# Attention with a gated MLP on one core: reciprocals spread over the partitions by DMA, and more heads with V stationary

## The chip, the cores and the metric

The kernel runs on one core of a Trainium2 chip. The metric is the device time of one execution in microseconds, the median of three runs. Its engines run side by side, each with its own queue of instructions, and wait for each other by semaphores: TensorE (PE, matmuls), VectorE (DVE), ScalarE (ACT), GpSimd (POOL) and SyncE (SP), which here only issues DMAs. Matmul results land in PSUM; everything else is in SBUF, which has 128 partitions.

## The reference

One row block of attention against a cached K and V, and an MLP that gates it; both read the same layer norm of x. There are 2048 queries, 2048 keys, 32 heads of 128, a model width of 512 and an MLP width of 1792; the types are bf16.

```python
xn = layernorm(x)                                   # [2048, 512]
q  = (xn @ wq)                                      # 32 heads x 128
scores = q @ k_cache.T * 128 ** -0.5                # per head [2048, 2048]
p  = softmax(scores)
o  = p @ v_cache                                    # per head [2048, 128]
s  = concat_heads(o) @ wo                           # [2048, 512]
h  = relu(xn @ w1 + b1) ** 2
g  = silu(h @ w2 + b2)
out = x + s * g
```

## The kernel before

The queries are worked in 4 blocks of 512; block and head together give 128 units, called heads here (g = 0 to 127). A head has 8 steps; each step takes two key tiles of 128. The scores are made transposed (keys on partitions), ScalarE takes the exponential of 128x1024 values into one of 8 buffers of pT, and the sum over keys is left to what follows. No maximum is subtracted. The Python program is a scheduler: it emits each engine's instructions in order, with estimated costs, and puts work without a fixed place (`calm`, `pool_quiet`, `sync_quiet`) where it expects the engine to be free.

```python
# scores of step pi (pi = 8 g + k), then the exponential into pT
for n in range(2):
    tt = 2 * k + n
    t = E(PE, partial(_mm, out=psA[...], lhsT=kT[:, i, tt * P:(tt + 1) * P], rhs=qt_sb[:, g % NQS, :], ...))
t_exp[pi] = E(AC, partial(_act, out=pT[:, pi % NPT, :], in_=psA[...], func=ACT.Exp, scale=SM_SCALE),
              deps=[t, t_PV[pi - NPT] ..., t_part.get(pi - NPT)])
```

P·V is made in one of two ways. In the first ("A", 16 heads before), pT is stationary and V, with a column of ones, moves: 64 matmuls of 129 columns a head. The denominators come out as the 129th column, in the queries' partitions; VectorE copies the result to o_un and takes reciprocals, GpSimd (VectorE for the last three heads) scales it to o_bf, and a transposing DMA makes oT.

In the second ("B", 112 heads before), V is stationary and pT moves: 16 matmuls of 512 columns. The result is already transposed (o_col, copied by ScalarE), but the denominators must be summed over partitions by other engines:

```python
def gen_pv_b(pi):
    ...
    for n in range(2):
        t_PV[pi] = E(PE, partial(_mm, out=bankO(b), lhsT=v_sb[:, i, tt, 0:Dh],
                                 rhs=pT[:, pi % NPT, n * QB:(n + 1) * QB], ...))
    if k == NPR - 1:
        t_free[b] = t_col[m] = E(AC, partial(_act, out=o_col[:, m % NOC, :], in_=bankO(b), func=ACT.Copy), ...)

# a step's sum over keys: either whole on VectorE ...
def den_part(pi):   # d_part 128x32 <- pT 128x1024, TRANSPOSE_TENSOR_REDUCE
# ... or GpSimd adds the two halves first, and VectorE reduces the sum
def part_add(pi):   # GpSimd: h_sum 128x512 <- pT[0:512] + pT[512:1024]
def part_half(pi, x):   # VectorE: d_part 128x16 <- h_sum 128x512

def den_sum(g):     # VectorE: d_sum 128x16 <- d_part
def den_write(g):   # DMA: d_scr (in DRAM) <- d_sum
def den_read(g):    # DMA: d_quad 128x(4x16) <- d_scr: each partition reads its four parts
def den_total(g):   # VectorE: d_rec 128x16 <- d_quad
def den_recip(g):   # VectorE: reciprocal in place
def den_spread(g):  # VectorE: r_all 128x512 <- d_rec, transposed in blocks of 32, each value repeated
    t_spr[m] = E(DV, partial(_transpose32, out=r_all[:], in_=spread),
                 deps=[t_rec[m], t_scale[m - 1] if m else None])
def den_scale(g):   # GpSimd: oT 128x512 <- o_col * r_all
    t_scale[m] = tok_oT[g] = E(GP, partial(_tt, out=oT[:, g % NOT, :], in0=o_col[:, m % NOC, :],
                        in1=r_all[:].rearrange("p b i -> p (b i)"), op=ALU.mult),
            deps=[t_col[m], t_spr[m], ...])
```

Which way a head takes is chosen when its turn comes, by the work that VectorE still owes:

```python
choose(g, FIRST_B <= g < NG - 3 and owed(pi) < OWED and (m < NOC or m - NOC in t_dr))
```

The first three and the last three heads are always of the first way. The products with wo, w1, w2 and wq fill the two psF banks between the steps. At the end the last four row tiles are made; they have two buffers z_t and two buffers out_t, the last tile in three pieces of 256, 128 and 128 columns:

```python
s = jt % 2
t = E(DV, partial(_stt, out=tmp_t[:, s, c0:c1], in0=place, scalar=0.5, in1=g_all[...], ...))      # z_t
t_fin[jt] = t_tmp[s] = E(eng, partial(_tt, out=out_t[:, s, c0:c1], in0=tmp_t[:, s, c0:c1],
                         in1=acc[:, qt, c0:c1], op=ALU.add), deps=[t, t_u[jt], t_outdma[s]])
dma = S.emit_dma(eng, partial(_dma, out=out[...], in_=out_t[:, s, c0:c1]), sl[s], deps=[t_fin[jt]])
```

Of the kernel before, what the change touches and what calls it, by code (L numbers as in the profile page):

```python
# [10 lines left out]
P = 128  # L11
# [73 lines left out]
def _uses_port(name, fn):  # L85
# [3 lines left out]
    if name == "DVE":  # L89
        if f in (_tt, _stt):  # L90
            return _in_sbuf(k["in0"]) and _in_sbuf(k["in1"])
        if f in (_ts, _copy):
# [6 lines left out]
          "d_quad": (1230, 4200)}  # L99
# [201 lines left out]
def bass_recurrent_scan__mha_block_cached__dense_activation_squared_relu__prompt_kernel(  # L301
# [40 lines left out]
    OWED = 9000  # L342
# [16 lines left out]
    NSL, NSW, NQS, NPT, NOT, NOC, NHS = 3, 4, 3, 8, 3 * HC, 3, 3  # L359
# [20 lines left out]
    d_sum = sb("d_sum", [P, 2, NBK], F32)  # L380
    d_quad = sb("d_quad", [P, 2, 4, NBK], F32)
    d_rec = sb("d_rec", [P, 2, NBK], F32)
    r_all = sb("r_all", [P, NBK, 32], F32)
    d_scr = nc.dram_tensor("d_scr", [2, 32, 4 * NBK], F32, kind="Internal").ap()
# [6 lines left out]
    x_ln = sb("x_ln", [P, TPB, D], BF16)  # L391
    xn_t = sb("xn_t", [P, TPB, D], BF16)
    st_t = sb("st_t", [P, TPB, 12], F32)
    mv_t = sb("mv_t", [P, TPB, 2], F32)
    nm_t = sb("nm_t", [P, TPB], F32)
# [3 lines left out]
    warm = sb("warm", [P, P], BF16)  # L399
# [33 lines left out]
    sl_dr = [S.slot(f"dr{i}") for i in range(2)]  # L433

# [22 lines left out]
    t_ones = None  # L457
    for i in range(NSL):
        t_ones = E(GP, partial(_memset, out=v_sb[:, i, :, Dh:Dh + 1], val=1.0))
# [12 lines left out]

    def ln_load(j, i, eng=SP):
        jt = j * TPB + i
        t_xl[jt] = S.emit_dma(
            eng, partial(_dma, out=x_ln[:, i, :], in_=A_x[0, jt * P:(jt + 1) * P, :]), sl_xl[i],
            deps=[t_xn.get(jt - TPB)])
# [3 lines left out]
    def ln_bn(j, i, c0=0, c1=D):  # L481
        jt = j * TPB + i
        k = 6 if c0 else 0
        t_bn[jt] = E(DV, partial(_bn_stats, out=st_t[:, i, k:k + 6], in_=x_ln[:, i, c0:c1]),
                     deps=[t_xl[jt], t_xn.get(jt - TPB), t_xr.get(jt - TPB)])
# [15 lines left out]
    def ln_scale(j, i):  # L501
        jt = j * TPB + i
        t_xn[jt] = E(DV, partial(_ts, out=xn_t[:, i, :], in0=x_ln[:, i, :],
                                 scalar1=mv_t[:, i, 0:1], scalar2=rstd[:, i:i + 1],
                                 op0=ALU.subtract, op1=ALU.mult),
                     deps=[t_xr[jt], t_xnr.get(jt - TPB)])

    def ln_transpose(j, i):
        jt = j * TPB + i
        t_xnr[jt] = tok_xT[j][i] = S.emit_dma(  # L510
            SP, partial(_dmaT, out=xnT[:, :, jt % (2 * TPB) * P:(jt % (2 * TPB) + 1) * P],
                        in_=xn_t[:, i, :]),
            sl_xT[i], deps=[t_xn[jt], t_xuse.get(j - 2)])
        assert j < 2 or n_xuse[j - 2] == NFC + H

    def ln_next(j, i):
        ln_scale(j, i)
        ln_transpose(j, i)

# [38 lines left out]
    def first_transpose(i):  # L558
        for c in range(NDC):
            t_xT[i] = E(PE, partial(_peT, out=bankF(1)[:, 0:256].bitcast(BF16)[:, c * P:(c + 1) * P],  # L560
                                    in_=xn_t[:, i, c * P:(c + 1) * P], ident=ident[:]),
                        deps=[t_xn[i], t_ident, tok_xT[0][i - 1] if i else None],
                        inc=(c == NDC - 1))
        t_xnr[i] = t_xT[i]
# [132 lines left out]
    t_sum = {}  # L697
    t_dw = {}
    t_dr = {}
# [60 lines left out]
    def den_sum(g):  # L760
        m = b_no[g]
        t_sum[m] = E(DV, partial(_reduce, out=d_sum[:, m % 2, :],
                                 in_=d_part[:, m % 2, 0:len(t_parts[g]), :].rearrange(
                                     "p n b -> p b n")),
                     deps=t_parts[g] + [t_dw[m - 2] if m >= 2 else None])

    def den_write(g):
        m = b_no[g]
        dst = bass.AP(tensor=d_scr.tensor, offset=d_scr.offset + m % 2 * P * NBK,
                      ap=[[NBK, 4], [4 * NBK, 32], [1, NBK]])  # L770
        t_dw[m] = S.emit_dma(SP, partial(_dma, out=dst, in_=d_sum[:, m % 2, :]), sl_dw[m % 2],
                             deps=[t_sum[m], t_dr[m - 2] if m >= 2 else None])

    def den_read(g):
        m = b_no[g]
        src = bass.AP(tensor=d_scr.tensor, offset=d_scr.offset + m % 2 * P * NBK,
                      ap=[[0, 4], [4 * NBK, 32], [1, 4 * NBK]])
        t_dr[m] = S.emit_dma(SP, partial(_dma, out=d_quad[:, m % 2].rearrange("p a b -> p (a b)"),
                                         in_=src), sl_dr[m % 2],
                             deps=[t_dw[m], t_tot[m - 2] if m >= 2 else None])  # L780

    def den_total(g):
        m = b_no[g]
        t_tot[m] = E(DV, partial(_reduce, out=d_rec[:, m % 2, :],
                                 in_=d_quad[:, m % 2].rearrange("p a b -> p b a")),
                     deps=[t_dr[m], t_spr.get(m - 2)])

    def den_recip(g):
        m = b_no[g]
        t_rec[m] = E(DV, partial(_recip, out=d_rec[:, m % 2, :], in_=d_rec[:, m % 2, :]),  # L790
                     deps=[t_tot[m]])

    def den_spread(g):
        m = b_no[g]
        base = d_rec[:, m % 2, :]
        spread = bass.AP(tensor=base.tensor, offset=base.offset,
                         ap=[list(base.ap[0]), [1, NBK], [0, 32]])
        t_spr[m] = E(DV, partial(_transpose32, out=r_all[:], in_=spread),
                     deps=[t_rec[m], t_scale[m - 1] if m else None])

    def den_scale(g):
        m = b_no[g]
        t_scale[m] = tok_oT[g] = E(
            GP, partial(_tt, out=oT[:, g % NOT, :], in0=o_col[:, m % NOC, :],
                        in1=r_all[:].rearrange("p b i -> p (b i)"), op=ALU.mult),
            deps=[t_col[m], t_spr[m], t_wodone[g - NOT] if g >= NOT else None])
# [5 lines left out]
    tiles = {}  # L812
    WEIGHT = {den_part: 1130, part_half: 610, den_sum: 350, den_total: 170, den_recip: 130,
              den_spread: 600}
# [4 lines left out]
    def plan_b(g):  # L819
        tiles[g] = 0  # L820
        first = NPR * g
        for k in range(NPR):
            calm(first + k + NPT - 2, partial(den_part, NPR * g + k))
        calm(first + NPR + 6, partial(den_sum, g))
        sync_quiet.append(partial(den_write, g))
        sync_quiet.append(partial(den_read, g))
        calm(first + NPR + 12, partial(den_total, g))
        calm(first + NPR + 12, partial(den_recip, g))
        calm(first + NPR + 13, partial(den_spread, g))
        pool_quiet.append(partial(den_scale, g))  # L830

    def needs(fn):
# [6 lines left out]
        if f in (den_sum, den_total, den_recip, den_spread, den_scale, den_write, den_read):  # L839
            g = a[0]  # L840
            m = b_no[g]
            if f is den_sum:
                if tiles[g] < NPR:
                    return None
                return t_parts[g] + [t_dw.get(m - 2) if m >= 2 else t_parts[g][0]]
            if f is den_write:
                return [t_sum.get(m), t_dr.get(m - 2) if m >= 2 else t_sum.get(m)]
            if f is den_read:
                return [t_dw.get(m), t_tot.get(m - 2) if m >= 2 else t_dw.get(m)]
            if f is den_total:  # L850
                return [t_dr.get(m), t_spr.get(m - 2) if m >= 2 else t_dr.get(m)]
            if f is den_recip:
                return [t_tot.get(m)]
            if f is den_spread:
                return [t_rec.get(m), t_scale.get(m - 1) if m else t_rec.get(m)]
            return [t_col.get(m), t_spr.get(m)]
# [17 lines left out]
    def ready_at(fn):  # L874
        toks = needs(fn)
        if toks is None or any(t is None for t in toks):
            return None
        slack = SLACK if fn.func in (den_total, den_read) else 0
        return S.ready(toks) + slack
# [25 lines left out]
    def fill_pool(until):  # L905
        while GP.t < until:
# [6 lines left out]
            if x < NHS or t_half[x - NHS] is not None:  # L913
# [125 lines left out]
    def at(step, fn):  # L1039
        events.setdefault(step, []).append(fn)  # L1040
# [86 lines left out]
    def job_wo(j, m, qt, c0=0, c1=D):  # L1127
# [16 lines left out]
        def evac(bank, step):  # L1144
# [14 lines left out]
            if last:  # L1159
# [5 lines left out]
                      deps=[box[0], t_g[jt], t_tmp[s], t_zrd[s]])  # L1165
                eng = GP if j == NQB - 1 and qt in (0, 2) else DV
                t_fin[jt] = t_tmp[s] = E(
                    eng, partial(_tt, out=out_t[:, s, c0:c1], in0=tmp_t[:, s, c0:c1],
                                 in1=acc[:, qt, c0:c1], op=ALU.add),
                    deps=[t, t_u[jt], t_outdma[s]])  # L1170
# [3 lines left out]
                                 in_=out_t[:, s, c0:c1]), sl[s], deps=[t_fin[jt]])  # L1174
# [5 lines left out]
    def load_xt(jt):  # L1180
        if jt < NQB * TPB:
            tok_xt[jt] = S.emit_dma(
                GP, partial(_dma, out=x_t[:, jt % 2, :], in_=A_x[0, jt * P:(jt + 1) * P, :]),
                sl_xt[jt % 2], deps=[t_u[jt - 2] if jt >= 2 else None])
# [141 lines left out]
    for j in range(NQB):  # L1326
        if j + 1 < NQB:
            for i in range(TPB):
                at(j * SPB + 3 * NPR, partial(ln_load, j + 1, i))
# [59 lines left out]
    t_bankF[:] = [t_q0[3], tok_xT[0][3]]  # L1389
    gen_pv(3)  # L1390
# [9 lines left out]
    for pi in range(NPAIR):  # L1400
        g, k = divmod(pi, NPR)
        if k == 0 and g > 0:
# [81 lines left out]
```

## Time and profile before

| | |
|---|---|
| median of 3 runs | 1221.58 us (1221.49 to 1221.91) |
| span of the profiled execution | 1219.6 us |
| TensorE busy | 1212.7 us |
| ScalarE, VectorE, GpSimd busy | 1088.4, 1076.8, 1067.4 us |
| moved by DMA | 174.83 MB, DMA engines busy about 0.7 of the span |

A line of the groups names the source line (often a helper's), the engine, the operation, what is written and read, the count, the busy time in us and the mean in ns of one; behind the second bar stands the idle time of the engine just before these instructions, and what ended it. The chain of waits follows the last instruction of the execution back to what released it, step by step; a piece of it is given as start, duration, engine and tile. Ends of matmuls are modelled, so a full TensorE is judged by the starts of its matmuls.

### The profile page before, as it was taken

Reading aid. Unit: us, or ns where it says so; the run is one execution under the profiler, and the core shown is the slowest. Engines: PE = TensorE matmul, PEld = TensorE weight load, DVE = VectorE, ACT = ScalarE, POOL = GpSimd, SP = SyncE. Lnnn points to the kernel's source line nnn. Section 1 sums busy time; section 2 is a strip of 40 time slices with the busy share of each in tenths; the row PEclk is TensorE's granted clock in tenths of the full one; section 3 lists DMA queues with packets and bytes.
Section 4 is the critical chain, followed back from the end, with each engine's and each line's share of the span. In section 5 each row is a group of like instructions: output and inputs, shape, how many; then the busy total and the mean of one; then the engine's idle time right before and its main releaser. Section 6 shows DMA issues by size and latency. Waiting matters only on the chain.

```text
span 1219.6 us, 19351 instructions
## 1 busy us (share of the span) xinstructions
PE 1212.7 (99%) x6509; PEld 588.5 (48%) x6509; DVE 1076.8 (88%) x1820; ACT 1088.4 (89%) x1156; POOL 1067.4 (88%) x978
## 2 busy tenths in 40 slices
PE   9999999999999999999999999999999999999998
PEld 7544444445454454444554444444454544444455
DVE  4798999898989888999999989898999899889983
ACT  7898999998988989999898999998989999989994
POOL 1789999998978989999888899999989789899971
PEclk9999999999999999999999999999999999999999
DMA  9998876667777666776687686766666686677651
GB/s 223 186 245 174 178 172 125 131 136 145 132 155 149 137 133 130 142 137 123 139 148 165 130 139 144 137 129 130 145 137 133 133 160 126 133 135 145 122 119 31
DMA packets 655492, 174.83 MB, mean 143 GB/s; under 512 B 642176, under 2 KB 654208, under 8 KB 655392
## 3 DMA queue, kind: packets, MB, share of 16 engines
q1 hardware_dynamic: 653296, 169.52, 70.4%
q0 software_dynamic: 1424, 3.81, 1.1%
q8 instruction: 52, 0.85, 0.3%
q14 instruction: 48, 0.39, 0.1%
q10 hardware_dynamic: 672, 0.26, 0.1%
HBM read 100.27 MB, written 3.01 MB: 85 GB/s over the span
## 4 chain that ended last, share of the span: by engine, by line
PE 96%; DVE 2%; POOL 1%; issue 0%; DMA 0%; ACT 0%; ACTq 0%; POOLq 0%; DVEq 0%
PE psA L226 35%; PE psO L226 31%; PE psF L226 25%; PE psO L231 4%; POOL h_sum L239 1%; DVE d_part L286 1%; DVE acc L249 0%; PE psA L231 0%; DMA out_dram<-out_t 0%; ACT pT L235 0%; DVE out_t L239 0%; POOL oT L239 0%; DVE z_t L249 0%; DVE acc L239 0%; PE psF L270 0%
## 5 line engine op out<-in xcount | busy, mean ns | idle before, releaser
L235 ACT ACTIVATE pT<-psA 128x1024 bf16<-128x1024 f32 x1024 | 1036.6, 1025 | 110.5 <-PE psA L226 71.8
L239 POOL TENSOR_TENSOR h_sum<-pT 128x512 f32<-128x512 bf16 x764 | 867.1, 1164 | 35.8 <-ACT pT L235 15.0
L226 PE MATMUL psA<-qt_sb,kT 128*128 128x512 bf16 x2032 | 604.5, 379 | 1.0 <-ACT pT L235 1.0
L286 DVE TRANSPOSE_TENSOR_REDUCE d_part<-h_sum 128x16 f32<-128x512 f32 x764 | 506.1, 685 | 31.8 <-POOL h_sum L239 29.3
L226 PE MATMUL psO<-pT,v_sb 128*128 128x512 bf16 x1792 | 533.0, 379 | 0.0
L226 PEld LDWEIGHTS psA<-qt_sb,kT 128*128 128x128 bf16 x2032 | 193.5, 98 | 213.1 <-ACT pT L235 4.3
L226 PEld LDWEIGHTS psO<-pT,v_sb 128*128 128x128 bf16 x1792 | 175.3, 98 | 211.4 <-issue 1.2
L239 POOL TENSOR_TENSOR oT<-o_col,r_all 128x512 bf16<-128x512 f32 x112 | 144.7, 1292 | 30.8 <-DVE r_all L290 30.4
L226 PE MATMUL psF<-xnT,wq_sb 128*128 128x512 bf16 (+1 forms) x520 | 168.9, 374 | 0.2 <-DVE xnT L253 0.2
L226 PE MATMUL psF<-wo_all,oT 128*128 128x512 bf16 x480 | 163.7, 379 | 0.0
L286 DVE TRANSPOSE_TENSOR_REDUCE d_part<-pT 128x32 f32<-128x1024 bf16 x132 | 159.1, 1212 | 4.5 <-ACT pT L235 4.1
L253 DVE CAST qt_sb<-psF 128x512 bf16<-128x512 f32 (+1 forms) x130 | 87.0, 669 | 23.4 <-PE psF L226 21.1
L231 PEld LDWEIGHTS psO<-v_sb,pT 128*128 128x128 bf16 x1024 | 68.1, 98 | 28.9 <-ACT pT L235 0.6
L226 PEld LDWEIGHTS psF<-xnT,wq_sb 128*128 128x128 bf16 x520 | 50.3, 98 | 60.0 <-issue 0.3
L231 PE MATMUL psO<-v_sb,pT 128*128 128x129 bf16 x1024 | 78.6, 220 | 0.3 <-ACT pT L235 0.3
L290 DVE STREAM_TRANSPOSE r_all<-d_rec 128x512 f32<-128x512 f32 x112 | 76.8, 686 | 0.5
L226 PE MATMUL psF<-xnT,w_sb 128*128 128x512 bf16 x224 | 77.1, 379 | 0.0
L226 PEld LDWEIGHTS psF<-wo_all,oT 128*128 128x128 bf16 x480 | 46.9, 98 | 56.4
L226 PE MATMUL psF<-w_sb,h2T 128*128 128x512 bf16 x224 | 73.6, 379 | 0.0
L235 ACT ACTIVATE o_col<-psO 128x512 f32<-128x512 f32 x112 | 66.3, 592 | 0.0
L245 DVE TENSOR_SCALAR r_t<-psF,b1f 128x512 bf16<-128x512 f32 x56 | 41.2, 735 | 15.6 <-PE psF L226 14.3
L282 DVE TENSOR_REDUCE d_sum<-d_part 128x16 f32<-128x144 f32 (+3 forms) x112 | 43.1, 385 | 1.1
(59 smaller groups left out, 404.5 us busy)
## 6 DMA issues: line engine op xcount, KB each, us to landing
v_sb<-in_A_v_cache_dram SPq DMA_DIRECT2D x127, 512.0 KB, 4.5
wq_sb<-in_A_wq_dram SPq DMA_DIRECT2D x127, 128.0 KB, 2.5
wo_all<-in_A_wo_dram SPq DMA_DIRECT2D x4, 1024.0 KB, 6.1
w_sb<-in_B_w_dram SPq DMA_DIRECT2D x14, 256.0 KB, 4.4
d_quad<-d_scr SPq DMA_DIRECT2D x112, 32.0 KB
x_t<-in_A_x_dram POOLq DMA_DIRECT2D x16, 128.0 KB, 3.5
kT<-in_A_k_cache_dram SPq DMA_TRANSPOSE x127, 4.7
x_ln<-in_A_x_dram SPq DMA_DIRECT2D x15, 128.0 KB, 3.0
```

What stands on the lines that cost most here:

```text
L226: return e.matmul(out, lhsT, rhs, start=start, stop=stop)
L231: return e.matmul(out, lhsT, rhs, start=start, stop=stop, skip_group_check=True)
L235: return e.activation(out, in_, func, bias=bias, scale=scale)
L239: return e.tensor_tensor(out, in0, in1, op)
L245: return e.tensor_scalar(out, in0, scalar1=scalar1, scalar2=scalar2, op0=op0, op1=op1)
L253: return e.tensor_copy(out, in_)
L282: return e.tensor_reduce(out, in_, axis=AX.X, op=ALU.add)
L286: return e.tensor_reduce(out, in_, axis=AX.X, op=ALU.add, apply_transpose=True)
L290: return e.transpose(out, in_)
```

## The change

In the way with V stationary the reciprocals no longer go to all partitions by a transpose on VectorE. The totals are made in 32 partitions only, one row per 16 queries; the reciprocals are written to a small array in DRAM (r_scr, one value per query) and read back by a second DMA that gives all 128 partitions the same 512 values. Before that, a small transpose on VectorE (128x32) makes d_sum's rows contiguous for its write. r_all gets two buffers, o_col four.

The constants of the scheduler are changed too: OWED from 9000 to 8000, GpSimd takes a step's sum only if VectorE owes more than 3500, and the estimates wait longer for the new reads. With them it chooses the second way for 118 heads in place of 112. To find room, the layer norm has two buffers in place of four (the first block's third and fourth tile borrow x_t and out_t), and the warm-up matmuls read o_bf. The last row tile's result goes to x_t, not to out_t, so that it has its own buffer.

```diff
-    NSL, NSW, NQS, NPT, NOT, NOC, NHS = 3, 4, 3, 8, 3 * HC, 3, 3
+    NSL, NSW, NQS, NPT, NOT, NOC, NHS = 3, 4, 3, 8, 3 * HC, 4, 3
-    OWED = 9000
+    OWED = 8000
+    POOL_OWED = 3500
+    HALF_SLACK = 600
...
+    def den_turn(g):
+        t_row[m] = E(DV, partial(_transpose32, out=d_row[:, m % 2, :], in_=d_sum[:, m % 2, :]),
+                     deps=[t_sum[m], t_dw.get(m - 2)])
...
     def den_read(g):
-        src = bass.AP(..., ap=[[0, 4], [4 * NBK, 32], [1, 4 * NBK]])
+        src = bass.AP(..., ap=[[NBK, 32], [32 * 32, 4], [1, NBK]])     # into 32 partitions
...
-    def den_spread(g):
-        t_spr[m] = E(DV, partial(_transpose32, out=r_all[:], in_=spread),
-                     deps=[t_rec[m], t_scale[m - 1] if m else None])
+    def rec_write(g):
+        t_rw[m] = S.emit_dma(SP, partial(_dma, out=r_scr[m % 2]..., in_=d_rec[0:32, m % 2, :]),
+            sl_rw[m % 2], deps=[t_rec[m], t_spr.get(m - 2)])
+    def rec_read(g):
+        src = bass.AP(tensor=r_scr.tensor, ..., ap=[[0, P], [1, QB]])
+        t_spr[m] = S.emit_dma(SP, partial(_dma, out=r_all[:, m % 2, :], in_=src), sl_rr[m % 2],
+                              deps=[t_rw[m], t_scale.get(m - 2)])
...
-            if x < NHS or t_half[x - NHS] is not None:
+            if (x < NHS or t_half[x - NHS] is not None) and owed(now[0]) > POOL_OWED:
...
+                end = jt == NQB * TPB - 1
+                row = (x_t if end else out_t)[:, s, c0:c1]
-                    eng, partial(_tt, out=out_t[:, s, c0:c1], in0=tmp_t[:, s, c0:c1],
+                    eng, partial(_tt, out=row, in0=tmp_t[:, s, c0:c1],
                                  in1=acc[:, qt, c0:c1], op=ALU.add),
-                    deps=[t, t_u[jt], t_outdma[s]])
+                    deps=[t, t_u[jt], None if end else t_outdma[s]])
```

## The prediction

> **What bounds the kernel now.** I read the page first: busy time and the slices, then the chain of work that ended last.
>
> ```profile
> PE 1212.7 (99%) x6509; PEld 588.5 (48%) x6509; DVE 1076.8 (88%) x1820; ACT 1088.4 (89%) x1156; POOL 1067.4 (88%) x978
> ...
> PEclk9999999999999999999999999999999999999999
> ...
> PE 96%; DVE 2%; POOL 1%; issue 0%; DMA 0%; ACT 0%; ACTq 0%; POOLq 0%; DVEq 0%
> PE psA L226 35%; PE psO L226 31%; PE psF L226 25%; PE psO L231 4%; POOL h_sum L239 1%; DVE d_part L286 1%; DVE acc L249 0%; PE psA L231 0%; DMA out_dram<-out_t 0%; ACT pT L235 0%; DVE out_t L239 0%; POOL oT L239 0%; DVE z_t L249 0%; DVE acc L239 0%; PE psF L270 0%
> ```
>
> TensorE is busy 99% of the span at the full clock and is 96% of the chain. A busy TensorE need not stream without gaps, so I took the starts of its matmul records in the trace. Start to start, a matmul with 512 columns takes 215.8 ns and one with 129 columns 56.7 ns. From 17 us on, only four gaps exceed the usual distance by over 30 ns: 0.10 us at 356, 1.20 us at 904.6, 0.05 us at 1182, 0.44 us at 1202.9. The stream of matmuls is the time; the rest is about 11 us of start and end. The other three engines, at 88 to 89%, count only where they make TensorE wait.
>
> Next the groups by line and shape, for the prices of what comes and goes (mean ns after the comma):
>
> ```profile
> L239 POOL TENSOR_TENSOR h_sum<-pT 128x512 f32<-128x512 bf16 x764 | 867.1, 1164 | 35.8 <-ACT pT L235 15.0 <-DVE d_part L286 13.9 <-DVE d_rec L257 2.7
> ...
> L286 DVE TRANSPOSE_TENSOR_REDUCE d_part<-pT 128x32 f32<-128x1024 bf16 x132 | 159.1, 1212 | 4.5 <-ACT pT L235 4.1
> L239 POOL TENSOR_TENSOR oT<-o_col,r_all 128x512 bf16<-128x512 f32 x112 | 144.7, 1292 | 30.8 <-DVE r_all L290 30.4
> ...
> L290 DVE STREAM_TRANSPOSE r_all<-d_rec 128x512 f32<-128x512 f32 x112 | 76.8, 686 | 0.5
> ...
> L235 ACT ACTIVATE o_col<-psO 128x512 f32<-128x512 f32 x112 | 66.3, 592 | 0.0
> ```
>
> The removed transpose costs VectorE 76.8 us in all, and GpSimd waits 30.4 us for it. Does TensorE ever wait for those? The chain in order of time, around its one long gap (start, us, what):
>
> ```profile
> 901.55 0.63 DVE r_all L290
> ...
> 902.26 1.15 POOL oT L239
> ...
> 903.49 1.16 POOL h_sum L239
> ...
> 904.73 1.03 ACT pT L235
> ...
> 905.81 0.60 PE psA L226 x2
> ```
>
> Once. VectorE was late with the spread of the reciprocals, GpSimd scaled late, hence added late, the exponential waited to overwrite that tile of pT, and the scores waited for the exponential: 1.2 us. Last, the end of the same chain:
>
> ```profile
> 1210.80 1.27 DVE out_t L239
> ...
> 1212.09 3.21 DMA out_dram<-out_t
> ...
> 1215.39 0.44 DVE out_t L239
> ...
> 1216.96 0.29 DVE out_t L239
> ```
>
> The last row tile has the buffer of the tile two before it, and its first piece waits until that tile's output DMA has landed (1215.30). TensorE's last matmul starts at 1215.12; the last VectorE result is there at 1217.25, its DMA is issued at 1217.28.
>
> **What the Trainium skill says.** (1) "TensorE: Matmul & The Clock Gate", section "Wait — 56ns, not 53.3ns?": warm matmuls follow each other at N ÷ 2.4 GHz plus about 2.5 ns. That makes 215.8 ns for 512 columns and 56.3 for 129; the trace has 215.8 and 56.7. It agrees. (2) "SBUF — State Buffer", section "Terms": VectorE and GpSimd take one port pair as an exclusive lock for a whole instruction, and the loser blocks. The trace agrees: GpSimd's out_t ran 1210.24 to 1211.51, and VectorE's out_t, begun at 1210.80, took 1262 ns in place of about 690. (3) "DMA: Bandwidth & Descriptors", section "Anatomy of one DMA — SWDGE (gpsimd) path": about 2 us per DMA are fixed, mostly the receipt of the write. The trace has something near on another queue: a read of d_scr that waits for its write is issued at the earliest 1.94 us after it.
>
> **The change part by part.**
>
> Six heads more with V stationary: 118 instead of 112. With pT stationary a head's P·V is 64 matmuls × 56.66 ns = 3.626 us; with V stationary 16 × 215.84 ns = 3.454 us. The difference is 0.173 us, and × 6 it is 1.04 us. It lies on TensorE, so it counts whole. Order and number of the other matmuls only move.
>
> VectorE: minus 112 transposes, 76.8 us. Minus 12 evictions o_un at 418 ns and 6 reciprocals at 163 ns, 6.0 us. Plus 118 transposes of 128x32 (den_turn); the nearest small VectorE rows, 230 and 234 ns for totals and reciprocals, make 0.17 us an estimate, 20 us. Plus 6 each of d_sum, total and reciprocal, 385 + 230 + 234 ns, 5 us. The built program has 764 half-tile sums (h_sum) as before, and 180 whole-tile sums on VectorE instead of 132: 48 × 1212 ns = 58.2 us. Total 1076.8 − 82.8 + 83.2 = about 1077 us. So all VectorE time won is spent on the six heads' denominators, and none of it shows as time.
>
> GpSimd: 6 × 1292 ns more for oT, 6 × 1040 ns less for o_bf: plus 1.5 us. ScalarE: 6 × 592 ns for o_col: plus 3.6 us. Neither becomes the bound; at 1092 and 1069 us they stay 120 us below TensorE.
>
> DMA: 118 reads of r_all, 128 rows of 2 KB = 256 KB each, 31 MB more on 175 MB; and 118 tiny writes of r_scr. The head's chain becomes write, read, total, reciprocal, write, read, scale. The added pair costs an estimated 5 to 6 us: 2 us for the write as for d_scr, 3 to 4 for the read, between the 3.0 us of the 128 KB x_ln and the 4.5 us of the 512 KB v_sb. A fourth o_col buffer covers that: a head lasts about 9.4 us, so one buffer more is worth more than the added latency. In SyncE's in-order queue the issues grow from 635 us (554 ns for a small one) by about 140 us. K is issued at the median 17 us, at the least 7.6 us, before its first use and lands in 4.7, so delays of 2 to 3 us stay hidden.
>
> The tail: the last tile's pieces write x_t, so the wait until 1215.30 is gone. Now the pieces follow TensorE, but the port lock stands in the way. GpSimd's sum for tile 14 runs 1213.55 to 1214.81. The first piece's z_t ends at 1214.01; its sum then blocks to 1214.81 and needs 0.28 us more (424 ns less the start-up that is hidden, as 547 of 690 ns remained in the earlier case): 1215.09. Then z_t, sum, z_t, sum at 0.33 us each: 1216.41. Against 1217.25 that is 0.84 us won. If VectorE is not blocked, the last piece follows the last matmul (1215.34 at the end) by 0.66 us, and 1.2 us are won.
>
> In sum: 1.04 + 0.84 = 1.9 us. 1221.6 − 1.9 = 1219.7. The gap of 1.2 us at 904 came through r_all on VectorE; I give it 6 in 10 to vanish (−0.7), and put +0.3 for new short gaps, since VectorE is as full as before. That is 1219.3 us.
>
> **The rivals.** (a) The freed 77 us shorten the kernel: then 1150 to 1200. The 99% of TensorE and four gaps of together 1.8 us speak against it; there is nothing to win beyond them. (b) The DMA takes the place of the transpose as a wait: GpSimd now waits for r_all to land, and as it runs in order, each late landing can repeat the gap of 904. SyncE already waited 115.6 us for d_scr to land. For it speaks the longer chain; against it, that the order puts the scale behind other sums (6 to 8 h_sum between two scales at the end), and that d_quad's landing cost VectorE only 0.6 us once. Ten such gaps would make 1231. (c) The tail gains nothing, because tile 14's output, in the old slot of tile 12, ends last: its DMA is issued at 1214.84 and lands about 2 us later, at 1216.8, before the last piece's, which would be issued at 1216.4. Then 0.84 us would shrink, not vanish: 1220. (d) The six heads fill VectorE so that evictions of psF and psO come late: a few gaps of 0.5 to 1 us, 1221 to 1224.
>
> **Range and chances.** The first two terms are sure to about 0.4 us, which makes 1219.3 to 1220.1 with the gap and 1218.1 to 1218.9 without it. Some new gaps stretch it upward. I take 1218.0 to 1221.3. Two per cent are 24 us; the floor of TensorE forbids it downward, and upward it takes twenty gaps like the one of 904. Hence 0.01 faster, 0.98 same, 0.01 slower.
>
> **What would show it.** TensorE at 99% and about 1 us less busy; 1888 matmuls psO with 512 columns and 640 with 129. VectorE near 1077 us, its STREAM_TRANSPOSE at about 0.17 us ×118, and 180 sums from pT. GpSimd's waits for r_all from VectorE gone, some for the DMA in their place. About 205 MB moved, a DMA share near 80%. At the end, the first piece of x_t stretched to about 1 us beside GpSimd's out_t. The prediction is wrong if waits of TensorE for ScalarE add up to over 2 us, or if GpSimd waits for r_all for tens of us and h_sum follows late.

## The result, and the profile after

The changed kernel takes 1225.01 us (median of 6 runs, 1223.39 to 1226.02) against 1221.53 us before (6 runs, 1221.28 to 1222.15). The ratio is 1.0026, with a 95% interval of 1.0013 to 1.0038: 3.5 us slower, where the prediction had 2.2 us faster. The spread is wider too: 2.6 us from the fastest to the slowest run of the changed kernel, 0.9 us before.

The page of the changed kernel, its busy times and the chain of work that ended last:

```profile
PE 1206.5 (99%) x6103; PEld 574.9 (47%) x6221; DVE 1083.0 (89%) x1874; ACT 1090.7 (89%) x1162; POOL 1066.4 (87%) x979
...
DMA packets 679300, 203.53 MB, mean 166 GB/s; under 512 B 650881, under 2 KB 662913, under 8 KB 679201
...
PE 79%; DVE 14%; POOL 3%; DMA 2%; issue 1%; ACT 1%; ACTq 0%; SPq 0%; POOLq 0%; DVEq 0%
PE psA L226 29%; PE psO L226 27%; PE psF L226 20%; DVE d_part L286 8%; POOL h_sum L239 3%; PE psO L231 2%; DVE acc L249 2%; DMA d_quad<-d_scr 1%; DVE qt_sb L253 1%; DVE d_sum L282 1%; ACT pT L235 0%; DVE acc L239 0%; DVE g_all L249 0%; DMA r_scr<-d_rec 0%; POOL oT L239 0%
```

TensorE is still busy 99%, but its share of the chain fell from 96% to 79%; VectorE rose from 2% to 14%. A busy share does not show this, the chain does. (Of 6221 matmuls 6103 have a record; each has its weight load, so the starts can still be read and the missing ones allowed for.) After the first 17 us TensorE's gaps, that is start-to-start distances less N/2.4 + 2.5 ns, add up to 7.7 us; before the change they were 2.3 us. The seven longest of over 0.45 us lie at 134 (0.47 us), 313 (2.12), 328 (0.56), 922 (0.59), 962 (1.00), 1163 (0.77) and 1183 (0.56).

Groups of the changed kernel, those that came or moved:

```profile
L239 POOL TENSOR_TENSOR oT<-o_col,r_all 128x512 bf16<-128x512 f32 x118 | 151.3, 1283 | 33.5 <-DMA r_all<-r_scr 32.0 <-DVE d_part L286 1.3
...
L249 DVE SCALAR_TENSOR_TENSOR acc<-acc,g_all 128x512 f32<-128x512 f32 x16 | 34.2, 2137 | 0.0
...
L282 DVE TENSOR_REDUCE d_rec<-d_quad 32x16 f32<-32x64 f32 x118 | 26.1, 221 | 12.4 <-DMA d_quad<-d_scr 12.3
L290 DVE STREAM_TRANSPOSE d_row<-d_sum 128x32 f32<-128x32 f32 x118 | 23.2, 197 | 2.4
```

The big transpose is gone and a 197 ns one has come. But VectorE now stands idle 12.3 us before the totals, waiting for d_quad to land, that is for its bytes to be there after the DMA was issued (0.6 us, once, before). And the 16 gate products acc = 0.5·acc·g_all, which the diff doesn't touch, cost 34.2 us instead of 26.0.

The chain of the changed kernel around the gap at 962 (start, us, what):

```profile
954.94 5.19 DMA d_quad<-d_scr
...
960.15 0.25 DVE d_rec L282
...
961.15 1.16 DVE d_part L286 x2
962.31 0.59 DVE z_t L249
...
962.95 0.39 PE psF L226
```

d_quad took 5.19 us to land. VectorE runs in order and waited; behind the wait stood the eviction of a psF bank (z_t), and TensorE waited for that bank. The gap at 134 has the same form, with a landing of 4.54 us at 117 and VectorE behind from then on.

The other kind, at 313: VectorE's and then GpSimd's timeline of the changed kernel (start, us, engine, instruction):

```profile
309.42 4.44 DVE L249 SCALAR_TENSOR_TENSOR acc<-acc,g_all 128x512 f32<-128x512 f32 x1
313.78 0.74 DVE L245 TENSOR_SCALAR r_t<-psF,b1f 128x512 bf16<-128x512 f32 x1
```

```profile
307.60 4.48 POOL L239 TENSOR_TENSOR h_sum<-pT 128x512 f32<-128x512 bf16 x4
312.05 1.26 POOL L239 TENSOR_TENSOR oT<-o_col,r_all 128x512 bf16<-128x512 f32 x1
313.94 1.15 POOL L239 TENSOR_TENSOR acc<-acc,x_t 128x512 f32<-128x512 f32 x1 [0.63 <-DVE acc L249]
```

A gate product that took 0.64 us at best took 4.44 us here: it ended 0.55 us after GpSimd's adds and the scale behind them had run through. Both have two operands in SBUF, and I read this as the fight for the shared port pair that the prediction describes. The eviction r_t behind it came late, and TensorE waited 2.1 us.

And the end, where the change did what it was meant to do (chain):

```profile
1214.22 3.92 PE psA L226 x26
...
1218.16 0.44 DVE z_t L249
...
1218.62 0.93 DVE x_t L239
...
1220.69 0.29 DVE x_t L239
```

The wait for the earlier tile's output is gone. The first piece stretched to 0.92 us beside GpSimd's out_t, as foreseen. From the start of TensorE's last matmul (1219.69) to the last VectorE result it is 1.29 us, against 2.13 us before.

### The profile page after: what moved, and what is told of

The parts are those of the page before. It is cut to its first block, busy times and chain, and to the rows that moved or that the text cites. A ratio compares the mean times of both kernels' runs of the same rounds, so it can differ in the third digit from the quotient of the medians.

```text
span 1222.9 us, 19101 instructions
## 1 busy us (share of the span) xinstructions
PE 1206.5 (99%) x6103; PEld 574.9 (47%) x6221; DVE 1083.0 (89%) x1874; ACT 1090.7 (89%) x1162; POOL 1066.4 (87%) x979
## 4 chain that ended last, share of the span: by engine, by line
PE 79%; DVE 14%; POOL 3%; DMA 2%; issue 1%; ACT 1%; ACTq 0%; SPq 0%; POOLq 0%; DVEq 0%
PE psA L226 29%; PE psO L226 27%; PE psF L226 20%; DVE d_part L286 8%; POOL h_sum L239 3%; PE psO L231 2%; DVE acc L249 2%; DMA d_quad<-d_scr 1%; DVE qt_sb L253 1%; DVE d_sum L282 1%; ACT pT L235 0%; DVE acc L239 0%; DVE g_all L249 0%; DMA r_scr<-d_rec 0%; POOL oT L239 0%
## 5 line engine op out<-in xcount | busy, mean ns | idle before, releaser
L226 PE MATMUL psA<-qt_sb,kT 128*128 128x512 bf16 x1980 | 593.3, 379 | 4.3 <-ACT pT L235 1.2
L226 PE MATMUL psO<-pT,v_sb 128*128 128x512 bf16 x1851 | 553.5, 379 | 1.9
L226 PEld LDWEIGHTS psO<-pT,v_sb 128*128 128x128 bf16 x1888 | 184.7, 98 | 222.2 <-issue 0.7
L286 DVE TRANSPOSE_TENSOR_REDUCE d_part<-pT 128x32 f32<-128x1024 bf16 x180 | 217.0, 1209 | 5.7 <-ACT pT L235 5.2
L239 POOL TENSOR_TENSOR oT<-o_col,r_all 128x512 bf16<-128x512 f32 x118 | 151.3, 1283 | 33.5 <-DMA r_all<-r_scr 32.0
L253 DVE CAST qt_sb<-psF 128x512 bf16<-128x512 f32 (+1 forms) x130 | 85.6, 659 | 21.9 <-PE psF L226 19.9
L231 PEld LDWEIGHTS psO<-v_sb,pT 128*128 128x128 bf16 x640 | 42.4, 98 | 17.6 <-ACT pT L235 0.6
L231 PE MATMUL psO<-v_sb,pT 128*128 128x129 bf16 x640 | 49.0, 220 | 0.3 <-ACT pT L235 0.3
L282 DVE TENSOR_REDUCE d_sum<-d_part 128x16 f32<-128x160 f32 (+3 forms) x118 | 46.6, 395 | 1.5
L249 DVE SCALAR_TENSOR_TENSOR h2T<-psF,b1f,r_t 128x512 bf16<-128x512 f32 x56 | 41.8, 747 | 1.7
```

The lines of the kernel that those rows point to most:

```text
L226: return e.matmul(out, lhsT, rhs, start=start, stop=stop)
L231: return e.matmul(out, lhsT, rhs, start=start, stop=stop, skip_group_check=True)
L239: return e.tensor_tensor(out, in0, in1, op)
L249: return e.scalar_tensor_tensor(out=out, in0=in0, scalar=scalar, in1=in1, op0=op0, op1=op1)
L253: return e.tensor_copy(out, in_)
L282: return e.tensor_reduce(out, in_, axis=AX.X, op=ALU.add)
```

## The experiments

Two theories stood first. L: landings are late, VectorE waits for d_quad in order and is then late with PSUM. F: the six more heads fill VectorE again, and that alone makes it late. The table has all runs; "waits" are those of VectorE for d_quad, "gate" is the time of the 16 gate products on VectorE, "gaps" are TensorE's after 17 us. These three are read in the profiled execution, which in e3, e5, e9 and e11 took 0.9 to 2.5 us more than the median. In all sessions the kernel before had medians of 1221.5 to 1221.8 us.

| run | heads with V stationary | us | ratio to before (95%) | waits us (times) | gate us | gaps us |
|---|---|---|---|---|---|---|
| before | 112 | 1221.53 | | 0.6 (1) | 26.0 | 2.3 |
| changed | 118 | 1225.01 | 1.0013 to 1.0038 | 12.3 (13) | 34.2 | 7.7 |
| e1_tail | 112 | 1220.40 | 0.9981 to 0.9997 | 0.2 (1) | 26.0 | 2.3 |
| e2_heads112 | 112 | 1227.05 | 1.0031 to 1.0055 | 21.6 (20) | 22.6 | 8.3 |
| e3_landing | 119 | 1231.46 | 1.0058 to 1.0089 | 4.0 (3) | 32.0 | 16.0 |
| e4_thin | 118 | 1220.36 | 0.9982 to 0.9994 | none | 30.4 | 3.2 |
| e5_gate | 118 | 1218.73 | 0.9964 to 0.9982 | 10.6 (10) | on GpSimd | 2.7 |
| e6_tail_gate | 112 | 1218.92 | 0.9968 to 0.9985 | none | on GpSimd | 1.0 |
| e7_half | 118 | 1219.51 | 0.9976 to 0.9990 | 5.8 (6) | 27.4 | 2.6 |
| e8_half_gate | 118 | 1217.99 | 0.9958 to 0.9981 | none | on GpSimd | 0.8 |
| e9_half_gate_112 | 112 | 1219.02 | 0.9971 to 0.9987 | 8.0 (9) | on GpSimd | 1.7 |
| e10_landing_gate | 119 | 1220.87 | 0.9984 to 1.0000 | 6.4 (7) | on GpSimd | 3.2 |
| e11_nogate | 118 | 1218.41 | 0.9971 to 0.9985 | 7.4 (9) | 19.1 | 3.8 |
| e12_thin112 | 112 | 1219.33 | 0.9977 to 0.9990 | 2.0 (5) | 19.9 | 1.0 |

**e1: the tail alone**, put into the kernel before.

```diff
+                end = jt == NQB * TPB - 1
+                row = (x_t if end else out_t)[:, s, c0:c1]
-                    deps=[t, t_u[jt], t_outdma[s]])
+                    deps=[t, t_u[jt], None if end else t_outdma[s]])
```

> The kernel before with one part of the change alone: the last row tile in its own buffer. Every theory: the wait for the landing of an earlier tile's output goes, 112 heads and four gaps of TensorE stay. From the last matmul's start to the end 3.2 us in place of 4.45 us; 1220.3 us in all (1219.9 to 1220.8).

1220.40 us, 1.36 us less than the kernel before beside it (1221.76). The gaps are those of before, even that at 904. So this part is a gain, and the loss comes from the rest.

**e2: 112 heads, everything else as changed.**

```diff
-            choose(g, FIRST_B <= g < NG - 3 and owed(pi) < OWED and ...)
+            choose(g, g not in [0, 1, 2, 8, 30, 36, 45, 62, 66, 73, 95, 102, 109, 125, 126, 127])
```

> The changed kernel with the same 112 heads as before with V stationary, all else as changed. Theory L (late landings: VectorE, in order, waits for d_quad, is then late with its PSUM evictions, and TensorE waits for the bank): the two more DMAs are still there, so waits for d_quad of about 12 us in all, gaps of TensorE of about 7 us, 1224 to 1226 us. Theory F (the six more heads fill VectorE again, and landings have little to do with it): gaps as before, about 2.3 us, and with the tail's gain 1220.0 to 1221.2 us.

1227.05 us: slower still, and above the range of L too. F falls in its simple form, as VectorE is less full here (busy 1036.6 us against 1083.0) and the kernel slower. The waits for d_quad went up to 21.6 us. Where VectorE has less queued work, the total comes up sooner after its read and more often finds it not landed: the median from landing to the total is 1.2 us here, 1.6 us in the changed kernel. The gate products took only 22.6 us here, less than before the change, so slower gate products didn't make these gaps. Not all come from d_quad: ahead of the one at 365 (1.06 us) GpSimd stood 6.4 us waiting for r_all.

**e4: the same order of instructions with little traffic.**

```diff
-                      ap=[[0, P], [1, QB]])
-        t_spr[m] = S.emit_dma(SP, partial(_dma, out=r_all[:, m % 2, :], in_=src), ...)
+                      ap=[[0, 8], [1, QB]])
+        t_spr[m] = S.emit_dma(SP, partial(_dma, out=r_all[0:8, m % 2, :], in_=src), ...)
```

> The changed kernel with every instruction of TensorE, VectorE and ScalarE in the same order, but r_all's read brings 8 of the 128 partitions only (16 KB in place of 256 KB; the others keep ones, so this leaves the scaling out there): 29 MB less on the DMA engines. L by traffic: d_quad lands as before the change (median 2.6 us in place of 3.25), VectorE's waits for it under 4 us, 1220 to 1222 us. L by SyncE's in-order queue (d_quad is issued late because SyncE stands waiting for r_scr): landings a little shorter, but the waits stay over 8 us and the time at 1223 to 1225 us. F: unchanged, 1224 to 1226 us.

1220.36 us, in the range of L by traffic. TensorE, VectorE and ScalarE have the very same sequence. From the view of the tile d_quad, first of the changed kernel, then of e4:

```profile
its engine sat idle before it (us, times) until:
  DMA d_quad<-d_scr: 12.3, 13
...
DMA to landing us min/median/max: 1.5/3.3/6.9
```

```profile
DMA to landing us min/median/max: 1.5/2.7/5.4
```

With 29 MB less on the DMA engines d_quad's landing falls from 3.3 to 2.7 us in the median (2.6 us before the change, where it was a read of 32 KB instead of 8), VectorE never waits for it, and of the seven long gaps five are gone. d_scr's landing falls too, from 2.9 to 1.9 us. SyncE's order is the same here, and the median from d_scr's landing to d_quad's issue is even longer (2.6 us against 1.3 us), so the gain did not come there. A part of the delay the queue has all the same: ahead of the changed kernel's gap at 1163, d_quad could be issued only when r_scr had landed (chain of the changed kernel):

```profile
1151.38 4.08 DMA r_scr<-d_rec
...
1155.85 3.27 DMA d_quad<-d_scr
...
1159.14 0.26 DVE d_rec L282
```

No run changed SyncE's order alone. The thin read also cut GpSimd's wait for r_all, from 32.0 to 9.5 us, so this run doesn't tell the two waits apart. What stays in e4 are the gap at 313, 1.8 us, with its gate product of 4.45 us, and the one behind it at 328, 0.57 us.

**e12: the thin read with e2's 112 heads**, both edits together; as in e4, the scaling of the other 120 partitions is left out.

> e2 (112 heads, changed chain, 1227 us) with the thin read of e4 and the same order of VectorE. If the bytes of r_all made e2 slow too: waits for d_quad fall from 21.6 us to under 8 us, TensorE's gaps from 8.3 to under 4 us, 1220.5 to 1222.5 us. If the order of 112 heads itself is bad: over 1224 us.

1219.33 us against e2's 1227.05: the traffic made e2 slow as well, and even more so. Waits 2.0 us, gaps 1.0 us. It came out below the range given.

**e7: half the bytes, the same rows.**

```diff
-    r_all = sb("r_all", [P, 2, QB], F32)
+    r_all = sb("r_all", [P, 2, QB], BF16)
-r_scr = nc.dram_tensor("r_scr", [2, QB], F32, kind="Internal").ap()
+r_scr = nc.dram_tensor("r_scr", [2, QB], BF16, kind="Internal").ap()
-        t_rec[m] = E(DV, partial(_recip, out=d_rec[0:32, m % 2, :], in_=d_rec[0:32, m % 2, :]),
+        t_rec[m] = E(DV, partial(_recip, out=d_inv[0:32, m % 2, :], in_=d_rec[0:32, m % 2, :]),
```

> The changed kernel with the same order of instructions, but reciprocals in bf16 from the reciprocal on: r_all's read is 128 KB in place of 256 KB, rows of 1 KB. If landings follow the bytes, this lies between the changed kernel and the thin read: d_quad's median 2.9 to 3.1 us, VectorE's waits for it 5 to 9 us, 1222 to 1223.5 us. If the count of rows matters and not the bytes (128 rows as before, the thin read had 8): as the changed kernel, 1224 to 1226 us.

d_quad's median of 3.0 us and VectorE's waits of 5.8 us lie in the ranges given, so the landings follow the bytes and not the count of rows. The time, 1219.51 us, is 2.5 us below the range, and below e4, which has no waits at all: time does not go with the sum of the waits. One thing more changed here: with r_all in bf16 GpSimd's scale takes 1167 ns in place of 1283, 13.8 us less in all, and the gate products 27.4 us in place of 34.2. How much of the gain is due to that isn't shown; the same holds for e8 and e9.

**e3: estimates of landings raised in the scheduler.**

```diff
-"d_scr": (530, 2200), "d_quad": (530, 4200), "r_scr": (530, 2200), "r_all": (1230, 4400)
+"d_scr": (430, 3000), "d_quad": (430, 5400), "r_scr": (580, 3300), "r_all": (350, 4400)
-    OWED = 8000
+    OWED = 9000
```

> The changed kernel with the scheduler's estimates of landings set near what its trace shows (d_scr 3.0, d_quad 5.4, r_scr 3.3 us; OWED back to 9000), 119 heads with V stationary: VectorE is fuller still, but its work that needs a landing stands later in its order. L: waits of VectorE for d_quad under 3 us in all, TensorE's gaps under 4 us, 1219.0 to 1221.5 us. F: gaps as in the changed kernel or longer, 1224 us or more.

Half a miss for L. The waits fell to 4.0 us (under 3 was expected), yet the time rose to 1231.46 us, with gaps of 16.0 us, of which some 3 us are half clock. Two gaps of 2.8 and 2.5 us stand behind gate products (2.2 us at 312, 2.4 us at 613) and late sums, and each was followed by 3.4 us at half clock (last section). So late landings are not the only cause, and a second theory came up: the fight for the port pair, in a VectorE that has no time left to catch up.

**e5 and e6: the gate products on GpSimd**, in the changed kernel and, with the tail, in the kernel before. The factor 0.5 moves into the evictions of acc. The heads with V stationary are fixed to those of the kernel that each starts from.

```diff
-                t_acc[qt] = t = E(DV, partial(_copy, out=acc[:, qt, :], in_=place),
+                t_acc[qt] = t = E(DV, partial(_ts, out=acc[:, qt, :], in0=place, scalar1=0.5, ...op0=ALU.mult),
-                t_acc[qt] = t = E(DV, partial(_tt, ... in1=acc[:, qt, :], op=ALU.add),
+                t_acc[qt] = t = E(DV, partial(_stt, ... scalar=0.5, in1=acc[:, qt, :], op0=ALU.mult, op1=ALU.add),
-        t_ug[jt] = E(DV, partial(_stt, out=acc[:, qt, :], in0=acc[:, qt, :], scalar=0.5, in1=g_all[...], ...),
+        t_ug[jt] = E(GP, partial(_tt, out=acc[:, qt, :], in0=acc[:, qt, :], in1=g_all[...], op=ALU.mult),
```

> The changed kernel, 118 heads, with the 16 gate products acc times g_all moved from VectorE to GpSimd (the factor 0.5 goes into the evictions of acc before them), so that they can't fight GpSimd for the port pair. The late landings stay. If the lock of 4.4 us at 309 made the 2.1 us gap there: that gap goes, the waits for d_quad stay near 12 us, TensorE's gaps fall from 7.7 to 5 to 6 us, 1222 to 1224 us. If the gap there was made by the landings too: it stays, 1224.5 to 1226 us.

> The kernel before (112 heads, reciprocals spread by VectorE) with the last tile's own buffer and the gate products on GpSimd. The gap of 1.2 us at 904 followed a gate product of 2.3 us; if the lock made it, it goes: TensorE's gaps 1.0 to 1.3 us in all, 1218.8 to 1219.6 us, faster than either kernel. If a full VectorE made it, it only moves: 1220 to 1221 us.

e5 comes to 1218.73 us, 6.3 us under the changed kernel and far below the range. The waits for landings are still there (waits of e5: who for whom, us, times, longest):

```profile
POOL oT L239 <- DMA r_all<-r_scr: 33.0, 14, 6.7
...
DVE d_rec L282 <- DMA d_quad<-d_scr: 10.6, 10, 2.2
```

10.6 us of waits on VectorE and 33.0 us on GpSimd cost little once the gate products are off VectorE: gaps 2.7 us. Most of what is left, 1.2 us at 250 to 258, stands behind another product of two SBUF operands on VectorE, g_all from th_t and z_t, that was not moved: one took 5.01 us, where the quickest took 0.62. e6 shows the same on the kernel before: the gap at 904 is gone, 1218.92 us as expected. In the chain of the kernel before, two gate products stood ahead of that gap:

```profile
891.78 2.98 DVE acc L249
...
897.52 2.22 DVE acc L249
```

**e11: the gate products cut to 8 of 512 columns, order unchanged.** e5 had changed VectorE's order as well (191 whole sums in place of 180); this run does not.

```diff
+    if out.tensor.name == "acc":
+        out, in0, in1 = out[:, 0:8], in0[:, 0:8], in1[:, 0:8]
```

> The changed kernel, every engine's instructions in the same order, full 256 KB reads, but each of the 16 gate products works on 8 of its 512 columns (this leaves the gate out of the other columns), so that it holds VectorE and the port pair for about 0.1 us. If the lock is the second cause beside the landings: waits for d_quad stay at 8 to 14 us, the gap of 2.1 us at 313 goes, 1219.5 to 1222 us. If the landings alone do it: the gap at 313 may go, but gaps at 134, 962 and 1163 stay and the time is 1222.5 us or more.

1218.41 us and waits of 7.4 us, both below the ranges: cutting the gate gives more than taking away the traffic (1220.36 in e4). But the products still took 19.1 us in all, in place of 34.2. At 0.15 and 0.64 us when free, that is an estimated 8 us less work and only 7 us less waiting, 17 us in place of 24, so this run doesn't tell how much of the gain is the lock. The gap at 313 halved (1.05 us) but stayed, and VectorE's and GpSimd's timelines of this run say why (this kernel's lines stand two lower):

```profile
309.53 3.91 DVE L251 SCALAR_TENSOR_TENSOR acc<-acc,g_all 128x8 f32<-128x8 f32 x1
```

```profile
307.72 4.47 POOL L239 TENSOR_TENSOR h_sum<-pT 128x512 f32<-128x512 bf16 x4
312.16 1.26 POOL L239 TENSOR_TENSOR oT<-o_col,r_all 128x512 bf16<-128x512 f32 x1
```

Eight columns, 146 ns when free, took 3.91 us. At this gap the wait costs, not the product. The runs of this kernel fall into two heaps, 13 of 21 from 1217.6 to 1218.8 us and 8 from 1220.3 to 1221.8; the profiled execution is of the upper one (1220.91 us). That one landing more or less decides a gap fits this, but isn't shown.

**e8, e9: both cures, with 118 and with 112 heads.** **e10: e3 with the gate on GpSimd.**

> Both in the changed kernel, 118 heads: bf16 reciprocals and the gate products on GpSimd. If the two causes add, TensorE's gaps come to 2 to 4 us and the time to 1219.5 to 1221.5 us. If VectorE is too full for 118 heads whatever is taken away (F), it stays over 1223 us.

> e8 (bf16 reciprocals, gate products on GpSimd) with the 112 heads of before in place of 118. With landings and lock out of the way, the six heads should be worth what their matmuls say, 6 x 0.173 = 1.04 us: TensorE's gaps under 1.5 us, 1218.7 to 1219.5 us. If 112 heads need other waits than 118 (as e2 was slower than the changed kernel), gaps of 3 us or more, over 1220.5 us.

> e3 (landing estimates near the trace, 119 heads, full 256 KB reads) with the gate products on GpSimd. In e3 the waits for d_quad were short (4.0 us) and the time was 1231 us all the same. If the lock of the gate products made its gaps: they fall from 16 us to under 3 us, 1217.5 to 1219.5 us. If 119 heads with the longer chain are too much for VectorE whatever the lock does: over 1222 us.

e8 is the fastest of all, 1217.99 us, below the range given, a ratio of 0.9969 to before. The page of e8, busy times and chain:

```profile
PE 1211.0 (100%) x6221; PEld 575.5 (47%) x6221; DVE 1058.0 (87%) x1858; ACT 1091.5 (90%) x1162; POOL 1058.2 (87%) x984
...
PE 99%; DMA 0%; DVE 0%; ACT 0%; ACTq 0%; SPq 0%; issue 0%; DVEq 0%
```

TensorE is 99% of the chain again, and the gaps are down to 0.8 us. The cures do not add (5.5 and 6.3 us alone, 7.0 us together): each removes nearly the same gaps. e9 is 1.03 us slower than e8, as six heads should cost. Against e6, which has the tail and the gate moved but the old transpose and 112 heads, the rest of the change is worth 0.9 us in e8 and 0.2 us in e5. e10 brings e3's gaps from 16.0 to 3.2 us, so most of them came with the gate on VectorE. Its 1220.87 us are above the range; with 119 heads and full reads some gaps stay.

## Why the prediction was wrong, point by point

- **Six heads more, 1.04 us on TensorE:** right in the size. e8 against e9 gives 1.03 us. That it is so close is partly luck: e9 still has 8.0 us of waits, and its profiled execution 0.9 us more gaps than e8's. The start of TensorE's last matmul less the gaps, 1212.3 us in e8 and 1213.1 in e9, gives 0.9.
- **The tail, 0.84 us:** right in its mechanism, with the stretched first piece (0.92 us), and to the last VectorE result exactly 0.84 us. The span's end gained 0.4 us more, as the span ended 1.9 us after that result instead of 2.3; e1 has 1.36 us in all.
- **VectorE stays full, at 1077 us:** 1083 us. The terms were right (d_part from pT 217 us; d_row 197 ns against an estimated 170). What was missing are 8 us more of gate products, by waiting and not by work.
- **DMA:** 203.5 MB and a share near 81%, as said; r_all lands in 3.8 us, as estimated. The write of r_scr was put too low: 3.2 us in the median, not 2, so the added pair takes about 7 us, not 5 to 6. SyncE's issues grew from 635 to 862 us, not by about 140. "Delays of 2 to 3 us stay hidden" was argued for K alone, and wasn't carried over to the small reads that share the DMA engines. There it fails. Before, nine tenths of the totals began 1.07 us or more after d_quad had landed; after the change that figure is 0.02 us, and in e4 1.16 us.
- **"+0.3 for new short gaps, since VectorE is as full as before":** this is the step that failed. The gaps went from 2.3 to 7.7 us, +5.4, where the prediction had −0.4 with its share for 904; without 904 the new gaps come to over 6 us. As full as before did not mean as much in time: d_quad came later, and the gate products lost more to GpSimd. Rival (b), the DMA as a wait in place of the transpose, was named, but put aside in part because "d_quad's landing cost VectorE only 0.6 us once", a figure of the old traffic. Its sign came true, 32.0 us of GpSimd's waits for r_all, but that wait is not what stood ahead of the long gaps in the changed kernel: their chains at 134, 962, 1163 and 1183 run through VectorE's total of a late d_quad, with evictions of PSUM behind it. One wait of 0.7 us for r_all stood ahead of a gap of 0.26 us at 928. e5 shows that neither wait costs much by itself: 10.6 and 33.0 us of them, and gaps of 2.7 us.
- **The gap at 904, "6 in 10 to vanish":** it shrank to 0.30 us, at 907, with r_all off VectorE and gate products of 3.21 and 2.43 us still ahead of it. But the reading of the chain was half of it: e6 keeps r_all on VectorE, moves the gate, and has no gap there. Taking away either was enough.
- **Rivals (a) and (c):** neither came about. No run gained more than 3.8 us on the kernel before, and the tail gained.
- **Rival (d), a full VectorE:** right in half. e2 shows that less work on it is no cure while the landings are late; e5 shows that waits for landings cost little once the gate products are off VectorE.

In sum the change gave 1.04 us on TensorE and 1.36 us at the end, and gave back some 5.4 us in gaps; 1221.5 − 2.4 + 5.4 = 1224.5, measured 1225.0. The two causes of the gaps work together: late d_quad landings, by r_all's traffic, and gate products that lose the port to GpSimd. Either removed brings the kernel below the one before. How far each gap belongs to one of them isn't settled: those at 134, 922, 1163 and 1183 vanish with the traffic alone (e4) and with the gate cut (e11). Nor is it shown that it is the port and not the mere work of the gate products that counts everywhere; for the gap at 313 the timelines speak for the port, and e2, with VectorE 46 us less busy and slower, speaks against mere work.

## What to carry to other kernels

Where one engine is full to 99%, the others' work isn't priced by its sum but by the delay it can put ahead of the evictions that the full engine waits for; look for what stands behind each wait in an in-order queue. More bytes on the DMA engines can lengthen the other transfers beside them, and slack measured under the old traffic is used up first: here the landing of wq_sb, which the change didn't touch, went from 2.5 to 3.4 us and that of kT from 4.7 to 5.1, while that of wo_all did not grow. An instruction with two SBUF operands on VectorE beside a GpSimd that adds back to back can cost the whole run of adds; here moving it to GpSimd helped. The additions to acc with one operand in PSUM never took more than 0.69 us in the changed kernel.

## What the runs showed of the hardware

The Trainium skill, "SBUF — State Buffer", section "Terms", says that the loser of the port pair blocks for the winner's instruction. The trace agrees and goes further: VectorE can lose several times in a row, with 4.44 us beside a run of adds and a scale in the changed kernel, and 3.91 us for a product of 8 columns in e11.

In the profiled execution of e3, gaps of 2.8 us at 317 and of 2.5 us at 622, with shorter ones near them, were each followed by a stretch at half the TensorE clock, 3.4 us long. The mean granted clock was 0.997 in three of e3's six runs and 1.0 in the others. The windows of e3 (us, busy time of each engine with its count, granted clock, DMA share, GB/s):

```profile
316.00:320.00 4.00, 1.60 (x17) 0.95 (x14) 4.00 (x6) 0.89 (x1) 3.48 (x3) 1.00 0.31 71
320.00:324.00 4.00, 3.59 (x23) 2.36 (x25) 3.58 (x8) 2.99 (x4) 0.00 (x0) 0.66 0.45 118
```

The 2.1 us gap of the changed kernel kept the full clock. The Trainium skill, "TensorE: Matmul & The Clock Gate", section "HAM oscillation — how this bites in real kernels", warns of idle gaps over about 3.4 us; here 2.5 us were enough, so that this gap cost more than its length.
